# A streamed weight slice loaded in two halves: halves of its columns in place of halves of its partitions

## The chip, the cores and the metric

The kernel runs on one NeuronCore of a Trainium2 chip. The metric is device time in microseconds, the median of several executions. One more execution was taken by the hardware profiler; every duration below is from it.

## The reference: what is computed

The output is a gated mix `g * a + (1 - g) * b` of two attention layers over the same 2048 tokens of width 640, all in bfloat16; `g` is a sigmoid of `x . gate_w` for each token.

Part B (`b`) is a local attention of 32 heads of 20 columns: each token looks at itself and at seven earlier tokens, two apart.

Part A (`a`) is recurrent. The tokens are cut into 64 segments of 32. A memory of 8 rows is put in front of each segment, giving 40 rows:

```python
for s in range(n_seg):                          # 64 segments
    h = concatenate([mem, x[segment s]])        # 40 rows of 640
    q, k, v = h @ Wq, h @ Wk, h @ Wv            # 640 -> 32 heads x 192, each
    p = softmax(mask(q @ k.T * scale))
    o = (p @ v) @ Wo                            # 32 x 192 -> 640
    mem = o[:8]                                 # goes into the next segment
    outs.append(o[8:])
```

Each of Wq, Wk, Wv is 640 x 6144 and Wo is 6144 x 640, some 31 MB in all, and every segment needs all of it. The segments can't be reordered, because each one's memory comes out of the one before.

## The kernel before

The weights are cut into 80 slices of 128 partitions x 1536 columns (384 KB each). A slice of Wq, Wk or Wv is 128 rows of the contraction (`kc`, five of them) by 1536 columns (`R`, four of them: eight heads each); a row of it in memory is 3072 contiguous bytes. Wo is cut by columns into `oa` (columns 0 to 255, a slice holds six chunks of 128 rows) and `ob` (columns 256 to 639, four chunks). 67 slices stay in SBUF; they are loaded once, on SP's queue, by whole slices (`slice_tile`, L407, and `load_late`, L421). The other 13 (`stream_keys`, L374, chosen evenly over the order of use) don't fit. They are streamed again in every segment through a pool of four buffers (`wstream`, `WBUFS` = 4, tile name `wst`). Three of the streamed slices belong to Wo and are first copied to a scratch tensor `wscr` (L392), where each partition's 1536 columns lie together. Ten slices are streamed once in the prepass too.

`get_slice` (L424) hands out a slice: a resident one, one that `begin` (L439) has loaded ahead, or a new `wst` buffer with its loads. The loads of a streamed slice are two DMAs (L434 to L436). All streamed loads are issued by SP's queue, one after the other. A load's issue waits until the matmuls that read the buffer's former slice are done. Other DMAs of a segment are issued by ACT's queue in ACT's own order: `load_z` (L577, `ZQKV<-zqk_dram`, 192 KB) after the first output copy, `oz_dram` (L808), the segment's output (L833), `load_vz` (L580, `ZQKV<-zv_dram`, 96 KB) after the first transposes, `a4` (L774) and `hT` (L573).

The time is spent in part A's loop (`part_a`, L585), one pass for each segment, of which the order on PE, ACT, DVE and SP is written out by hand. On PE a pass is: `m_dense` for q and k (L588: four matmuls for each slice, one for each 32-column tile `j` of the array, 384 columns of the slice each, so that tile 0 reads columns 0 to 383, tile 3 reads 1152 to 1535); `t_qk`, transposes (L621); scores (`s_a`, `s_b`, L640 and L649); `m_v` in between; the products with v (`pv_half`, L696 and L700); then `o_group` (L726), which multiplies by Wo in 48 chunks, four at a time on the four column tiles. ACT and DVE copy PSUM to SBUF between these steps (L602, L624, L625, L709, L805, L815) and do the softmax. When two matmuls in a row use the same stationary operand, `drop_loads` (L27) removes the second weight load.

Before the loop, `part_b` computes `b` into a scratch tensor, and `prepass` computes the q, k and v parts of the 8 last rows of all segments together. After it, `part_z` (L864) computes the output rows that were held back, from slices that are still in SBUF.

Of the kernel before, what the change touches and what calls it, by code (L numbers as in the profile page):

```python
# [45 lines left out]
class _K:  # L46
# [377 lines left out]
    def get_slice(self, key):  # L424
        if key in self.res_tiles:
            return self.res_tiles[key]
        if key in self.ahead:
            return self.ahead.pop(key)
        src, split = self.slice_info(key)
        t = self.wstream.tile([128, 1536], BF, name="wst", tag="wst")  # L430
        v = t if split is None else t.rearrange("p (c f) -> p c f", c=split[0])
        if key in self.wscr:
            src = self.wscr[key].rearrange("p (c f) -> p c f", c=split[0])
        for x in range(2):  # L434
            part = slice(64 * x, 64 * x + 64)
            self.nc.sync.dma_start(v[part], src[part])  # L436
        return v

    def begin(self, *keys):  # L439
# [508 lines left out]
```

## Time and profile before

| | |
|---|---|
| runs | 2179.46, 2170.18, 2177.9 us; median 2177.9 |
| profiled execution | 2179.46 us; span from first to last instruction 2177.7 us |
| PE, matmul | 1747.3 us busy (80%) |
| DVE, ACT | 655.2 us (30%), 687.5 us (32%) |
| DMA | 434.65 MB, mean 200 GB/s; 273170 packets |
| SP's DMA queue | 183336 packets, 380.54 MB, 69.4% of 16 engines' span |
| granted TensorE clock | 0.954 |
| streamed loads | 520 of Wk, 520 of Wv, 384 of `wscr`, 260 of Wq, 192 KB each |

How to read the profile. The page lists the busy time of each engine (PE is the matmul, PEld the weight load of TensorE; POOL is GpSimd; SP issues DMAs and computes nothing) and the span in 40 equal slices, each digit a busy share in tenths. The row DMA is the mean busy share of the 16 DMA engines, GB/s is what they moved. A DMA moves its bytes as packets, one for each contiguous row here. A view by windows gives the busy time of each engine in a stretch of time (us from the start of the span), with the number of instructions in brackets, and in its last columns the granted clock, the DMA share and GB/s. A view of waits says which engine stood idle at which line until what ended: us in total, times, longest. `PE ps_d_5073 L594` is a matmul of line 594 into that PSUM tile, `SPq` the DMA queue of SP. The chain follows the work that ended last backwards, each step to what released it; a DMA in it runs from its issue to its landing.

### The profile page before, as it was taken

The numbers are of one execution on the slowest core, as the hardware profiler recorded it, in microseconds if no ns is written. First come the engines' busy times: TensorE is split into PE (matmuls) and PEld (weight loads), VectorE is DVE, ScalarE is ACT, GpSimd is POOL, SyncE is SP. The second block draws the span as 40 slices with busy tenths as digits, with TensorE's granted clock in tenths as the row PEclk, the third lists the DMA queues.
The fourth block names the chain that finished last, engine by engine and source line by source line (L and its number), as shares of the span: only waits on it lengthen the run. The fifth ranks groups of instructions, "written<-read, shape, count | busy, mean of one in ns | idle before, by whom it ended". The sixth has DMA issues, their size and how long they took to land.

```text
span 2177.7 us, 81473 instructions
## 1 busy us (share of the span) xinstructions
PE 1747.3 (80%) x42085; PEld 785.3 (36%) x30693; DVE 655.2 (30%) x1614; ACT 687.5 (32%) x1436; POOL 30.7 (1%) x62
## 2 busy tenths in 40 slices
PE   6989998777788778777877877777777787777778
PEld 3555443233333333323333333333333333333337
DVE  4555222222222232222222222222222222222221
ACT  5666221223222232222222232223223222322230
POOL 4000000000000000000000000000000000000000
PEclk9999999899998999999999999999999999999999
DMA  9111869898888899888888888889888888888891
GB/s 300 37 27 37 260 181 258 205 213 212 212 209 206 209 218 220 211 213 204 215 210 214 216 217 210 205 212 216 212 208 217 212 210 216 212 213 216 212 254 54
DMA packets 273170, 434.65 MB, mean 200 GB/s; under 512 B 101804, under 2 KB 158644, under 8 KB 272820
## 3 DMA queue, kind: packets, MB, share of 16 engines
q1 hardware_dynamic: 183336, 380.54, 69.4%
q10 hardware_dynamic: 89484, 48.90, 9.7%
q8 instruction: 286, 4.69, 1.0%
q14 instruction: 64, 0.52, 0.1%
HBM read 395.62 MB, written 34.86 MB: 198 GB/s over the span
## 4 chain that ended last, share of the span: by engine, by line
DMA 56%; PE 31%; SPq 4%; ACT 4%; issue 3%; DVE 1%; POOL 1%; ACTq 0%; DVEq 0%
DMA wst<-in_A_Wv_dram 18%; DMA ZQKV<-zqk_dram 12%; DMA wst<-in_A_Wk_dram 11%; DMA wst<-wscr 9%; PE ps_d_5073 L594 4%; SPq L436 4%; PE ps_d_5074 L732 4%; PE ps_d_5075 L732 3%; PE ps_d_5075 L594 3%; DMA ZQKV<-zv_dram 3%; PE ps_bqk L236 2%; ACT bP L259 2%; DMA wst<-in_A_Wq_dram 2%; PE ps_d_5075 L880 1%; PE ps_d_5073 L880 1%
## 5 line engine op out<-in xcount | busy, mean ns | idle before, releaser
L594 PEld LDWEIGHTS <-hT 128*32 128x32 bf16 x5632 | 163.8, 97 | 578.6 <-issue 491.2
L594 PE MATMUL ps_d_5073<-wst,hT 128*32 128x384 bf16 x1280 | 121.3, 349 | 209.0 <-DMA wst<-in_A_Wv_dram 93.2
L602 DVE CAST ZQKV<-ps_d_5075 128x768 bf16<-128x768 f32 x128 | 122.6, 958 | 291.1 <-PE ps_d_5075 L594 288.4
L732 PEld LDWEIGHTS <-ZQKV 128*32 128x32 bf16 x4608 | 138.6, 101 | 144.7 <-DMA wst<-wscr 61.0
L732 PE MATMUL ps_d_5075<-zs_4166,ZQKV 128*32 128x384 bf16 x1792 | 168.3, 357 | 0.4 <-issue 0.4
L594 PE MATMUL ps_d_5075<-wst,hT 128*32 128x384 bf16 x1024 | 91.4, 332 | 88.9 <-DMA wst<-in_A_Wv_dram 43.2
L621 PEld LDWEIGHTS <-ZQKV 128*128 128x128 bf16 x1536 | 89.0, 100 | 202.6 <-issue 156.8
L732 PE MATMUL ps_d_5074<-zs_4166,ZQKV 128*32 128x256 bf16 x2304 | 146.3, 290 | 3.8 <-issue 3.6
L625 ACT COPY ZQKV<-ps_d_5075 128x768 bf16<-128x768 bf16 x64 | 51.2, 800 | 225.1 <-PE ps_d_5075 L621 225.1
L602 DVE CAST ZQKV<-ps_d_5073 128x768 bf16<-128x768 f32 x64 | 61.3, 958 | 184.6 <-PE ps_d_5073 L594 184.6
L602 ACT CAST ZQKV<-ps_d_5074 128x768 bf16<-128x768 f32 x64 | 51.2, 799 | 205.3 <-PE ps_d_5074 L594 205.3
L732 PE MATMUL ps_d_5074<-wst,ZQKV 128*32 128x256 bf16 x768 | 78.2, 299 | 26.9 <-DMA wst<-wscr 26.0
L640 PEld LDWEIGHTS <-ZQKV 128*32 128x32 bf16 (+1 forms) x4096 | 57.6, 93 | 101.3 <-issue 65.8
L625 ACT COPY ZQKV<-ps_d_5073 128x768 bf16<-128x768 bf16 x64 | 51.2, 800 | 123.6 <-PE ps_d_5074 L669 94.5
L709 DVE CAST ZQKV<-ps_d_5073 128x192 bf16<-128x192 f32 x128 | 39.8, 353 | 162.4 <-PE ps_d_5073 L700 162.4
L709 ACT CAST ZQKV<-ps_d_5074 128x384 bf16<-128x384 f32 x64 | 30.7, 480 | 179.5 <-PE ps_d_5072 L667 85.7
L602 ACT CAST ZQKV<-ps_d_5072 128x768 bf16<-128x768 f32 x64 | 51.2, 799 | 113.3 <-PE ps_d_5072 L594 99.5
L709 DVE CAST ZQKV<-ps_d_5075 128x384 bf16<-128x384 f32 x64 | 35.7, 558 | 145.6 <-PE ps_d_5075 L700 71.1
L624 DVE COPY ZQKV<-ps_d_5074 128x768 bf16<-128x768 bf16 x64 | 35.7, 558 | 137.0 <-PE ps_d_5074 L621 137.0
L732 PE MATMUL ps_d_5075<-zv_4165,ZQKV 128*32 128x384 bf16 x1024 | 73.6, 329 | 1.6 <-issue 1.6
L696 PEld LDWEIGHTS <-ZQKV 32*128 32x128 bf16 (+1 forms) x4096 | 44.4, 101 | 79.4 <-issue 63.0
L709 ACT CAST ZQKV<-ps_d_5072 128x192 bf16<-128x192 f32 x128 | 34.7, 322 | 109.9 <-PE ps_d_5073 L700 109.9
(639 smaller groups left out, 3955.2 us busy)
## 6 DMA issues: line engine op xcount, KB each, us to landing
wst<-in_A_Wk_dram SPq DMA_DIRECT2D x520, 192.0 KB
wst<-in_A_Wv_dram SPq DMA_DIRECT2D x520, 192.0 KB
wst<-wscr SPq DMA_DIRECT2D x384, 192.0 KB
wst<-in_A_Wq_dram SPq DMA_DIRECT2D x260, 192.0 KB
zqk_dram<-zs_4166 ACTq DMA_DIRECT2D x4, 3072.0 KB
ZQKV<-zqk_dram ACTq DMA_DIRECT2D x64, 192.0 KB
zv_dram<-zv_4165 SPq DMA_DIRECT2D x32, 192.0 KB
ZQKV<-zv_dram ACTq DMA_DIRECT2D x64, 96.0 KB
```

The source lines that it names most:

```text
L236: nc.tensor.matmul(ps[:, 0:nn], lhsT=wqk[n][:, kc, 4 * g:4 * g + 4, :].rearrange("p h d -> p (h d)"), rhs=xT[:, kc, o0:o0 + nn], start=(kc ...
L259: nc.scalar.activation(Pv, ps[0:nk, :, 0:nq * nu], ACT.Exp, scale=scale_b)
L436: self.nc.sync.dma_start(v[part], src[part])
L594: mm = nc.tensor.matmul(dst[x // 2][32 * j:32 * j + 32, x % 2, 0:384], lhsT=hT[:, kc, :], rhs=sl[:, 384 * j:384 * j + 384], start=(kc == 0 ...
L602: cp(KV[:, 384 * u:384 * u + 768].rearrange("p (a f) -> p a f", a=2), ps[:, :, 0:384])
L621: nc.tensor.transpose(p[:, r, t, :], unit[2 * r + m][:, 128 * t:128 * t + 128], self.ident[:])
L625: nc.scalar.copy(KV[:, 4 * 384:6 * 384].rearrange("p (c b i) -> p c b i", b=4, i=8), blocks(pk))
L640: nc.tensor.matmul(pSs[h][32 * j:32 * j + 32, par, 40 * r:40 * r + 40], lhsT=KT[R][k0:k1, c, :], rhs=q_blocks(R)[k0:k1, :, c, :], start=(r ...
L696: nc.tensor.matmul(out[:, r, t, :], lhsT=V[2 * h + r][ks, f0:f1], rhs=E[ks, par, 40 * r:40 * r + 40], start=(r == 0 and t == 0), stop=Fals ...
L709: cp(dst, src[:, :, :, 8:40])
L732: mm = nc.tensor.matmul(b_out[part][32 * jj:32 * jj + 32, 0:n], lhsT=oTxs[2 * (R // 2) + j // 2][:, 6 * (j % 2) + 3 * (R % 2) + t, :], rhs ...
L880: nc.tensor.matmul(ps[32 * q:32 * q + 32, 0:nf], lhsT=oz[n, q][:, 24 * (R // 2) + 6 * j + 3 * (R % 2) + t, :], rhs=wo[part, c // nc_][:, c ...
```

## The change

A streamed slice is still loaded by two DMAs of 192 KB into the same buffer. Before, the first took partitions 0 to 63 with all 1536 columns and the second partitions 64 to 127. After, both take all 128 partitions: the first takes columns 0 to 767, the second columns 768 to 1535. For the slices of Wo the columns are counted in chunks (`split[0]`): three and three for `oa`, two and two for `ob`, which are 768 columns as well. A row of one DMA is 1536 bytes instead of 3072, and there are 128 of them instead of 64. A matmul contracts over all 128 partitions, so before it needed both DMAs. After, the matmuls of column tiles 0 and 1 read columns of the first DMA alone, those of tiles 2 and 3 of the second.

```diff
--- before.py
+++ after.py
@@ -432,8 +432,8 @@
         if key in self.wscr:
             src = self.wscr[key].rearrange("p (c f) -> p c f", c=split[0])
         for x in range(2):
-            part = slice(64 * x, 64 * x + 64)
-            self.nc.sync.dma_start(v[part], src[part])
+            part = slice(768 * x, 768 * x + 768) if split is None else slice(split[0] // 2 * x, split[0] // 2 * (x + 1))
+            self.nc.sync.dma_start(v[:, part], src[:, part])
         return v
 
     def begin(self, *keys):
```

## The prediction

> **What bounds the kernel now.** I read the page first: who is busy, and what the DMA engines do over the span.
>
> ```profile
> PE 1747.3 (80%) x42085; PEld 785.3 (36%) x30693; DVE 655.2 (30%) x1614; ACT 687.5 (32%) x1436; POOL 30.7 (1%) x62
> ...
> DMA  9111869898888899888888888889888888888891
> ...
> q1 hardware_dynamic: 183336, 380.54, 69.4%
> ```
>
> No engine is full, but from slice 10 to 38, the 64 segments of part A, the DMA engines are 80 to 90% busy. Next, the busy time of stretches I chose: x and B's weights (rows of 1280 B) arriving; resident slices (128 partitions, rows of 3072 B); late Wo slices (128 partitions, rows of 512 and 768 B); streamed slices; then 56 segments.
>
> ```profile
> core 0: us, PE busy (x) PEld busy (x) DVE busy (x) ACT busy (x) POOL busy (x), PEclk, DMA share, GB/s
> 5.00:10.00 5.00, 3.75 (x29) 2.74 (x30) 0.18 (x1) 2.74 (x5) 0.00 (x0) 1.00 1.00 343
> 233.00:247.00 14.00, 14.00 (x67) 6.30 (x66) 4.58 (x2) 2.11 (x2) 0.00 (x0) 1.00 1.03 396
> 360.00:370.00 10.00, 10.00 (x48) 4.51 (x46) 1.76 (x1) 2.88 (x2) 0.00 (x0) 1.00 1.00 290
> 440.00:450.00 10.00, 8.95 (x254) 3.69 (x201) 2.42 (x10) 3.31 (x10) 0.00 (x0) 0.83 1.03 235
> 500.00:2000.00 1500.00, 1174.70 (x32386) 487.79 (x22442) 421.63 (x1173) 436.18 (x1005) 0.00 (x0) 0.95 0.88 212
> ```
>
> The last two columns matter. With all 16 DMA engines full, 128-partition loads move 290 to 396 GB/s; the streamed halves, 64 partitions with the long 3072 B row, move 235 (247 in a short full stretch at 1023). The same row is 1.6 times dearer when a DMA covers half the partitions. The last row gives the segment: 1500 / 56 = 26.8 us, PE busy 1174.7 / 56 = 21.0, idle 5.8. The waits of PE in the same 56 segments say for what:
>
> ```profile
> PE ps_d_5073 L594 <- DMA wst<-in_A_Wv_dram: 86.4, 73, 4.0
> PE ps_d_5073 L594 <- DMA wst<-in_A_Wk_dram: 54.8, 55, 2.2
> PE ps_d_5073 L594 <- DMA wst<-in_A_Wq_dram: 42.4, 84, 1.7
> PE ps_d_5075 L594 <- DMA wst<-in_A_Wk_dram: 36.2, 54, 1.5
> PE ps_d_5075 L594 <- DMA wst<-in_A_Wv_dram: 27.2, 53, 1.4
> PE ps_d_5074 L732 <- DMA wst<-wscr: 23.1, 44, 1.3
> ```
>
> Together 270.1 us, 4.8 a segment: nearly all of PE's idle time is for streamed halves. The waits of SP, which issues them, over the same stretch:
>
> ```profile
> SPq L436 <- DMA ZQKV<-zv_dram: 190.9, 54, 5.4
> SPq L436 <- DMA ZQKV<-zqk_dram: 152.0, 56, 4.4
> ```
>
> A streamed half shares no data with those loads. But all DMAs of SP and ACT take turns on eight completion semaphores (283 or 284 issues on each in the trace), so an issue waits for the landing of the one eight back. 26 halves and six ACT DMAs make 32 a segment, four rounds exactly: the same half always stands behind the same load. Last, the chain, around one segment (start, us, what):
>
> ```profile
> 1014.00 5.40 DMA ZQKV<-zqk_dram
> 1019.41 3.14 DMA wst<-in_A_Wk_dram
> ...
> 1031.08 5.37 DMA wst<-in_A_Wv_dram
> 1036.49 1.47 PE ps_d_5073 L594 x13
> ```
>
> A DMA issued into a full queue takes 5.4 us; one issued when SP's wait had let the queue drain takes 3.14. That 2.3 us of standing in line recurs, and is itself made of half-rate transfers.
>
> **The change part by part.** Number, size and order of the DMAs stay (1684 of 192 KB); the shape changes.
>
> (1) Transfer. Before: 196.6 KB at 235 to 247 GB/s, 0.82 us a half. After: 128 rows of 1536 B. The trace before has no steady load of that form; 290 GB/s (rows of 512 and 768 B) bounds it below and 396 (3072 B) above, 0.68 and 0.50 us. I take 0.57, from 343 GB/s at 1280 B, the nearest row length. A segment has 26: 21.3 us become 14.8 (13.0 to 17.7). Other DMA work stays: 0.88 x 26.8 = 23.6, less 21.3, is 2.3. The DMA engines' need falls from 23.6 to 17.1 us (15.3 to 20.0), below PE's 21.0 at either end. Nothing is added to the bytes.
>
> [...]
>
> [...]
>
> (2) SP. One issue takes 465 to 588 ns at L436 (medians); 128-partition issues at L421 took 430 for plain rows and 657 for Wo in three dimensions. I take no change, 0 to +0.1 us each, at most 2.6 us a segment, hidden while SP waits 3.5 and 2.7 us a segment for the two loads above. Without that cover, the halves behind it would be late by as much; that end is inside (4).
>
> (3) Waits of PE. The first matmul of a slice waited for both halves; now column tiles 0 and 1 (in Wo: the first half of the chunks) wait for the first, 2 and 3 for the second. Behind a waiting matmul stands all of PE's queue, and behind that the evictions of ACT and DVE. The first pair can start up to one pace (0.6 us) earlier, the end still needs the second half: 0, between -0.1 and +0.05 us a slice (-1.3 to +0.65 a segment), in the same bounds. SP's reuse wait on PE splits likewise: the first half of a buffer is free two matmuls (some 0.2 us) sooner. 0.
>
> (4) The loop, by the timeline and SP's waits of one segment, from one zqk issue (1014.00) to the next (1041.61): zqk lands at +5.4 and lets a Wk half go, landed +8.55; transposes; ACT issues zv at +9.9; SP, free at +11.0, waits 3.9 and resumes at +15.0; its fourth issue is the Wv half at +17.1, landed +22.45; PE then needs 5.1 to the next zqk. With the line gone, a load takes what the drained one took: zqk 3.3 (oz goes beside it), Wk 3.1, +1.3 to zv, zv 3.3, 2.1 for SP's issues, Wv 3.1, 5.1 of PE: 21.3 instead of 27.6, 6.3 shorter. PE's own busy time in that stretch is 21.3 too. So stalls cannot all remain, and what is late next is PE itself.
>
> (5) The segment: 26.8 - 4.8 = 22.0 if all named stalls went. Two limits of almost one length take turns, and ACT's and DVE's evictions, now covered by stalls, come out in part (PE's loads already wait 38.8 us at L621 for L657, 0.7 a segment): +1.0, between 0 and 2.5 (half the stall left). The granted clock is 0.95 over the segments, 0.74 in the 5 us after the 1031-to-1036 stall, but 1.00 in the prepass where PE never rests. With fewer stalls I take half of 5% of 21.0: -0.5, between 0 and -1.0. Sum: 22.5 (21.0 to 24.5), 4.3 less, times 64: 275.
>
> (6) Start and prepass: single stalls on the stream, 7.6 us on Wv before 470 us the largest: -10 (0 to -15). Part B and the end hold no streamed slice.
>
> 2179.5 (this execution; span 2177.7) - 275 - 10 = 1894; the median of the runs is 1.6 lower: 1893. Own range: 2178 - 64 x 5.8 - 15 = 1792 to 2178 - 64 x 2.3 = 2031.
>
> **The rivals.**
> A. The stream is faster, but eight semaphores, four buffers and SP's pace stay the bound. For: SP's two waits, 6.1 us a segment; SP needs 26 x 0.57 = 14.8 more, 20.9 in all. Against: those waits are for transfers that are late through the line itself. More than half of the stall stays: 1.0 to 2.3 us gained a segment, 2114 to 2031, say 2070.
> B. The change doesn't do what it says: a row of 1536 B costs half of today's 3072 B row, as if the line were at the memory and not at the partitions. For: zqk's 1536 B rows go no faster while halves stream. Against: 396 GB/s from the same tensors, same stride. Then 0.82 us stays: 2170 to 2185.
> [...]
>
> **How the numbers follow.** Forecast 0.70, A 0.20, B 0.04, C 0.06. A measurement of this kernel tells 0.5%, 11 us. Forecast and A are faster: 0.90; B same: 0.04; C slower: 0.06. The range leaves out C and B, a tail of A above 2060 and the lowest tenth of the forecast: 1810 to 2060.
>
> **What would show it.** Packets on the first queue rise by 107776 to 291112 (rows doubled) at equal bytes. DMA share falls to some 0.76 (17.1 / 22.5) while GB/s rises to about 253 (212 x 26.8 / 22.5). The zqk and zv waits of SP fall below 2 us each; the 5.4 us pieces of the chain go to about 3.3 and PE lines rise in it; PE is busy over 90% of a segment. Wrong: a DMA share still at 0.88 (B, C), or PE still idle over 2.5 us a segment at a low share (A).

## The result, and the profile after

The changed kernel takes 1759.9 us (median of four runs, 1754.9 to 1767.1) against 2178.7 for the kernel before: a ratio of 0.8085, with a 95% interval of 0.8047 to 0.8122. The direction and the first cause of the forecast, cheaper halves, hold; the time lies 133 us under its number and 50 us under its range. The profiled execution took 1761.2 us, with a span of 1759.5.

The page of the changed kernel, the same three lines as before:

```profile
PE 1614.6 (92%) x42085; PEld 768.7 (44%) x30693; DVE 652.9 (37%) x1614; ACT 684.1 (39%) x1436; POOL 30.7 (2%) x62
...
DMA  9300185978889999889998989988989899988981
...
q1 hardware_dynamic: 291112, 380.54, 68.1%
```

The bytes are the same and the packets are 107776 more, as the doubled rows demand. The DMA engines are still 90% busy in part A, but the span has shrunk. The surprise is in the first line: PE does the same 42085 matmuls in 1614.6 us of busy time instead of 1747.3.

The window of 56 whole segments (from one zqk load to another; columns as before, the last three being granted clock, DMA share and GB/s):

```profile
core 0: us, PE busy (x) PEld busy (x) DVE busy (x) ACT busy (x) POOL busy (x), PEclk, DMA share, GB/s
459.50:1588.20 1128.70, 1051.95 (x32488) 463.05 (x22516) 420.98 (x1176) 434.65 (x1009) 0.00 (x0) 1.00 0.90 283
```

A segment is 1128.70 / 56 = 20.16 us instead of 26.8; PE is busy 18.8 of them (21.0 before) and idle 1.4 (5.8 before). So of the 6.7 us that a segment lost, 4.4 were idle time and 2.2 were busy time. 283 GB/s pass where 212 did.

The longest waits of PE in that window, and SP's longest waits, with those for the two loads that held it up before (whole span):

```profile
PE ps_d_5074 L732 <- issue: 14.9, 17, 1.6
PE ps_d_5075 L594 <- DMA wst<-in_A_Wk_dram: 7.2, 9, 1.3
PE ps_d_5073 L594 <- DMA wst<-in_A_Wk_dram: 6.5, 13, 1.2
PE ps_d_5075 L594 <- DMA wst<-in_A_Wv_dram: 6.4, 17, 1.1
...
```

```profile
SPq L436 <- DMA wst<-in_A_Wv_dram: 90.7, 108, 2.6
SPq L436 <- PE ps_d_5073 L594: 90.3, 162, 1.7
SPq L436 <- DMA wst<-in_A_Wk_dram: 83.1, 108, 3.5
...
SPq L436 <- DMA ZQKV<-zqk_dram: 7.2, 12, 1.1
...
SPq L436 <- DMA ZQKV<-zv_dram: 5.5, 7, 1.8
```

All waits of PE on `wst` in these 56 segments come to 30.7 us, 0.55 a segment, where the six rows shown before had 270. SP hardly waits for zqk and zv now. In the 56 segments it waits 240 us, 4.3 a segment, for matmuls to free a buffer; there it runs as far ahead as four buffers allow. But 168 us, 3.0 a segment, go to the landing of its own earlier halves (135 us, 2.4 a segment, from 500 to 2000 us of the kernel before): SP's and ACT's issues take turns on eight completion semaphores in this trace too, 283 or 284 on each, and an issue still waits for the DMA eight places back.

Last, the chain around one segment:

```profile
1022.56 5.83 DMA wst<-in_A_Wk_dram
1028.43 0.34 PE ps_d_5075 L594 x2
1028.82 0.43 SPq L436
1029.36 0.36 SPq L436
1029.77 4.51 DMA wst<-in_A_Wv_dram
1035.53 1.09 PE ps_d_5075 L594 x24
```

A load still takes 4.5 to 5.8 us from issue to landing. The line in front of the DMA engines didn't go away; it is only served faster. The chain of this profile can be followed back to 861 us only. In the 898 us that it covers, DMAs make some 27% of it and PE 63%; before, where it covers the whole span, they made 56% and 31%.

### The profile page after: what moved, and what is told of

Read it like the earlier page. It is cut to its first block, busy times and chain, and to the rows that moved or that the text cites. A ratio compares the mean times of both kernels' runs of the same rounds, so it can differ in the third digit from the quotient of the medians.

```text
span 1759.5 us, 80890 instructions
## 1 busy us (share of the span) xinstructions
PE 1614.6 (92%) x42085; PEld 768.7 (44%) x30693; DVE 652.9 (37%) x1614; ACT 684.1 (39%) x1436; POOL 30.7 (2%) x62
## 4 chain that ended last, share of the span: by engine, by line
PE 32%; DMA 14%; issue 2%; SPq 1%; ACT 1%; ACTq 1%; DVE 0%
PE ps_d_5073 L594 6%; DMA wst<-in_A_Wk_dram 6%; DMA wst<-in_A_Wv_dram 5%; PE ps_d_5075 L594 5%; PE ps_d_5075 L732 3%; PE ps_d_5074 L732 3%; PE ps_d_5072 L594 2%; PE ps_d_5074 L594 2%; PE ps_d_5075 L880 2%; PE ps_d_5073 L880 1%; DMA wst<-in_A_Wq_dram 1%; SPq L436 1%; DMA wst<-wscr 1%; PE ps_d_5072 L621 1%; PE ps_d_5074 L696 1%
## 5 line engine op out<-in xcount | busy, mean ns | idle before, releaser
L594 PEld LDWEIGHTS <-hT 128*32 128x32 bf16 x5632 | 160.6, 96 | 363.2 <-issue 266.3
L732 PEld LDWEIGHTS <-ZQKV 128*32 128x32 bf16 x4608 | 126.6, 96 | 109.0 <-issue 56.5
L594 PE MATMUL ps_d_5073<-wst,hT 128*32 128x384 bf16 x1280 | 128.7, 330 | 15.7 <-DMA wst<-in_A_Wk_dram 7.6
L732 PE MATMUL ps_d_5075<-zs_4166,ZQKV 128*32 128x384 bf16 x1792 | 141.4, 327 | 0.6 <-issue 0.6
L732 PE MATMUL ps_d_5074<-zs_4166,ZQKV 128*32 128x256 bf16 x2304 | 132.4, 276 | 8.8 <-issue 8.2
L602 ACT CAST ZQKV<-ps_d_5074 128x768 bf16<-128x768 f32 x64 | 51.2, 800 | 199.0 <-PE ps_d_5074 L594 179.5
L594 PE MATMUL ps_d_5075<-wst,hT 128*32 128x384 bf16 x1024 | 101.9, 328 | 25.2 <-DMA wst<-in_A_Wv_dram 17.4
L625 ACT COPY ZQKV<-ps_d_5075 128x768 bf16<-128x768 bf16 x64 | 51.2, 800 | 119.0 <-PE ps_d_5075 L621 119.0
L625 ACT COPY ZQKV<-ps_d_5073 128x768 bf16<-128x768 bf16 x64 | 51.2, 800 | 95.4 <-PE ps_d_5074 L669 45.9
L640 PEld LDWEIGHTS <-ZQKV 128*32 128x32 bf16 (+1 forms) x4096 | 53.6, 92 | 64.4 <-issue 34.8
L602 ACT CAST ZQKV<-ps_d_5072 128x768 bf16<-128x768 f32 x64 | 51.2, 800 | 70.0 <-DMA wst<-in_A_Wv_dram 38.7
L732 PE MATMUL ps_d_5075<-zv_4165,ZQKV 128*32 128x384 bf16 x1024 | 71.4, 326 | 2.1 <-issue 2.0
L709 ACT CAST ZQKV<-ps_d_5074 128x384 bf16<-128x384 f32 x64 | 30.7, 480 | 92.3 <-PE ps_d_5072 L667 77.9
L259 ACT ACTIVATE bP<-ps_bS 128x968 bf16<-128x968 f32 (+1 forms) x80 | 64.8, 856 | 3.9 <-PE ps_bS L254 3.8
```

Of the source, the lines that this page charges most:

```text
L259: nc.scalar.activation(Pv, ps[0:nk, :, 0:nq * nu], ACT.Exp, scale=scale_b)
L594: mm = nc.tensor.matmul(dst[x // 2][32 * j:32 * j + 32, x % 2, 0:384], lhsT=hT[:, kc, :], rhs=sl[:, 384 * j:384 * j + 384], start=(kc == 0 ...
L602: cp(KV[:, 384 * u:384 * u + 768].rearrange("p (a f) -> p a f", a=2), ps[:, :, 0:384])
L625: nc.scalar.copy(KV[:, 4 * 384:6 * 384].rearrange("p (c b i) -> p c b i", b=4, i=8), blocks(pk))
L640: nc.tensor.matmul(pSs[h][32 * j:32 * j + 32, par, 40 * r:40 * r + 40], lhsT=KT[R][k0:k1, c, :], rhs=q_blocks(R)[k0:k1, :, c, :], start=(r ...
L709: cp(dst, src[:, :, :, 8:40])
```

## The experiments

Theory P: what pays is that each DMA covers all 128 partitions. Rival W: what pays is the other half of the edit, that column tiles 0 and 1 can start before the slice is complete. Theory S, formed after the result, is on the surprise: stalls lengthen PE's busy time too.

**The early start taken away (second_first).** The changed kernel, with the half that the first matmul needs issued last:

```diff
-        for x in range(2):
+        for x in (1, 0):
```

> The changed kernel with the two column halves issued in the other order: columns 768 to 1535 first, columns 0 to 767 second. The first matmul of a slice (column tile 0) now waits for the half that is issued last, so nothing of a slice can start before all of it has landed; the transfers stay the same. Theory P (it is the 128-partition shape of each DMA that pays): 1760 to 1775 us, PE's waits on wst up by less than 20 us in all. Rival W (it is the early start of column tiles 0 and 1 that pays): 0.5 to 0.8 us come back for each slice that PE waits for, 13 a segment at most, so 1850 us or more.

1758.4 us (1752.1 to 1759.9); on its own chip a ratio of 0.8116 (0.8095 to 0.8137) to the kernel before, where the changed kernel has 0.8085 (0.8047 to 0.8122). PE's waits on `wst` rise from 30.7 to 43.1 us in 56 segments, and nothing comes of it in the time. Rival W falls: the halves' separate waits are worth nothing here that can be measured.

**One DMA for a slice (whole_slice, and again beside the changed kernel).**

```diff
-        for x in range(2):
-            part = slice(768 * x, 768 * x + 768) if split is None else slice(split[0] // 2 * x, split[0] // 2 * (x + 1))
-            self.nc.sync.dma_start(v[:, part], src[:, part])
+        self.nc.sync.dma_start(v[:], src)
```

> The changed kernel with one DMA for a streamed slice: 128 partitions, all 1536 columns, rows of 3072 B, 384 KB. It has the row length of the kernel before, the partition span of the changed kernel and no early start. Theory P: rows of 3072 B as cheap as the resident ones (396 GB/s), SP issues 13 instead of 26 a segment, 1745 to 1790 us. Rival W: PE waits for whole slices as in the kernel before, 1850 us or more. Rival C (short rows): if 1536 B rows cost extra, this is clearly faster than the changed kernel, under 1740 us.

> The changed kernel unaltered, on the same chip as the next two, so that their difference is read directly: 1750 to 1770 us.

> One DMA of 384 KB for a streamed slice again, beside the changed kernel on one chip. If the 2% of the first comparison is real: 1715 to 1735 us, 25 to 45 us under the changed kernel.

1724.1 us in the first comparison. That is under the 1745 to 1790 us expected, and in the range put down for dear short rows (under 1740). On one chip: the changed kernel 1753.9 us, ratio to the kernel before 0.8035 (0.8008 to 0.8062); whole slices 1723.3 us, ratio 0.7888 (0.7862 to 0.7913). The gain of some 2% is real, and this version beats both kernels. No half at all is needed, which speaks against W a second time. The window of 56 segments of the version with whole slices:

```profile
457.00:1557.00 1100.00, 1031.85 (x32488) 453.24 (x22512) 421.32 (x1176) 434.33 (x1009) 0.00 (x0) 1.00 0.89 290
```

19.64 us a segment; the DMA engines need 0.89 x 19.64 = 17.5 us, against 0.90 x 20.16 = 18.1 with halves. Rows of 3072 B are thus a little cheaper than twice as many of 1536 B, though with (17.5 - 2.2) / 13 = 1.18 us a slice (334 GB/s; the 2.2 us of other DMA work are from the kernel without a stream below) not as cheap as the 396 expected. SP also issues half as often and waits 1.4 us a segment for its own loads to land instead of 3.0, and PE's waits on `wst` fall to 6.6 us. Which of these makes the 2% wasn't separated.

**Rows halved once more (rows_768).**

```diff
+        if split is None:
+            v4, s4 = (a.rearrange("p (j f) -> p j f", f=384) for a in (v, src))
+        else:
+            v4, s4 = v, src
         for x in range(2):
-            part = slice(768 * x, 768 * x + 768) if split is None else slice(split[0] // 2 * x, split[0] // 2 * (x + 1))
-            self.nc.sync.dma_start(v[:, part], src[:, part])
+            self.nc.sync.dma_start(v4[:, x::2, :], s4[:, x::2, :])
```

> The changed kernel with halves made of every other 384 columns (column tiles 0 and 2, then 1 and 3; in Wo every other chunk): still two DMAs of 192 KB over 128 partitions, but rows of 768 B (512 B in slices of the first 256 columns of Wo), twice as many. Theory P: a row's price follows its bytes (768 B rows took half of 1536 B rows in the first traces), the DMA need rises by 5 to 20% from the 290 GB/s that such rows made before, 1770 to 1850 us. Rival C: each row costs a fixed amount and this doubles it again; DMA share at 1.0 and over 1900 us.

1812.4 us (1805.4 to 1817.9), ratio 0.8361 (0.8330 to 0.8392). The packets of SP's queue rise to 539432, the DMA need to 19.3 us a segment (0.92 of 20.94). Short rows cost, but only 6% more need for twice the rows: a row's price is nearly its bytes. A half takes (19.3 - 2.2) / 26 = 0.66 us here, still under the 0.82 us of the kernel before.

**The disputed price alone (late_low_first, late_mid_first).** 25 resident slices that are loaded before the prepass, each in halves of 64 partitions. In dispute is why streamed halves move 235 GB/s where whole resident slices move 396: by P1 it is which partitions one DMA touches, P2 and P3 are the rivals below. The two kernels differ in which partitions go first (the diff is the first one's; the other has `[[(32, 96)], [(0, 32), (96, 128)]]`):

```diff
+        todo = []
...
-            self.nc.sync.dma_start(v, src)
             self.res_tiles[k] = v
+            todo.append((v, src))
+        for group in [[(0, 64)], [(64, 128)]] if part == 0 else [[(0, 128)]]:
+            for v, src in todo:
+                for a, b in group:
+                    self.nc.sync.dma_start(v[a:b], src[a:b])
```

> The changed kernel with the 25 slices of the first late load (before the prepass) each loaded in two DMAs of 64 partitions: all low halves (partitions 0 to 63) first, then all high halves. No PE work waits for them in between, so the DMA rate at full share is read directly between 230 and 275 us. [...] Rival P2 (the streamed halves were slow because low and high halves alternate, or because of the PE's reads): 380 GB/s or more.

> As the former, but the first DMA of each slice takes partitions 32 to 95, and the rest (0 to 31 and 96 to 127) follow in a second pass. The first pass has the same DMAs as to size (192 KB), row count (64) and row length (3072 B); only the partitions differ. [...] Rival P3 (64 rows in one DMA are too few for 16 engines, four each): 230 to 250 GB/s in the first pass too.

The whole kernels take 1774.1 and 1780.9 us (one execution each). Windows of the first pass, partitions 0 to 63 first:

```profile
core 0: us, PE busy (x) PEld busy (x) DVE busy (x) ACT busy (x) POOL busy (x), PEclk, DMA share, GB/s
235.00:240.00 5.00, 4.95 (x24) 2.29 (x24) 0.66 (x1) 1.86 (x1) 0.00 (x0) 1.00 1.06 205
240.00:245.00 5.00, 5.00 (x25) 2.28 (x24) 2.29 (x1) 0.00 (x0) 0.00 (x0) 1.00 1.05 202
245.00:250.00 5.00, 4.95 (x24) 2.25 (x23) 0.00 (x0) 1.86 (x1) 0.00 (x0) 1.00 1.05 207
```

and partitions 32 to 95 first:

```profile
230.00:235.00 5.00, 5.00 (x25) 2.29 (x24) 0.61 (x1) 1.83 (x1) 0.00 (x0) 1.00 0.93 298
235.00:240.00 5.00, 4.95 (x24) 2.26 (x24) 1.68 (x1) 1.44 (x1) 0.00 (x0) 1.00 0.87 294
240.00:245.00 5.00, 5.00 (x25) 2.25 (x23) 2.13 (x1) 0.42 (x1) 0.00 (x0) 1.00 0.82 262
```

The same 192 KB, the same 64 rows of 3072 B: 204 GB/s with the engines full, against up to 298 with the engines not even full. The first is under the 235 of the streamed halves, the second under the 396 of whole slices. In the second, SP issued one such DMA only every 0.64 us, which is 307 GB/s at most; the price itself is in the packet records of the trace. A 3072 B packet takes 251 ns (median; mean 249) for partitions 0 to 63 and 121 ns (mean 146) for 32 to 95. In the changed kernel, which loads these slices whole, it is 121 ns (mean 126). With a mean of 146 ns, 16 engines move 337 GB/s at most, so the issue alone didn't keep the second kernel from 396. The means of 249, 146 and 126 ns leave most of the price to which partitions a DMA touches, and little to its size or the number of its rows: P2 and P3 fall. Low halves alone are even dearer than low and high in turn (200 ns in the loop of the kernel before).

The second passes add little. The high halves, 64 to 127, moved 200 to 213 GB/s with the engines full, as dear as the low ones. The pieces 0 to 31 and 96 to 127 moved 207 to 213 GB/s at a DMA share of 0.70 to 0.74: SP issued one of these 96 KB DMAs every 0.465 us, which is 211 GB/s, so they don't tell the price with the engines full.

What makes 0 to 63 and 64 to 127 dear and 32 to 95 not is not shown by these runs.

**PE's busy time without stalls (no_stream, before_six).** In both, streamed slices are replaced by resident ones of the same matrix after the first segment: all 13 in the changed kernel, seven of 13 in the kernel before (there the diff's last condition is `i % 2 == 0`).

```diff
+        if key in self.alias:
+            return self.res_tiles[self.alias[key]]
...
+            gone = [k for i, k in enumerate(k for k in self.slice_keys() if k in self.stream_keys) if True]
+            self.alias = {k: next(r for r in self.res_tiles if r[0] == k[0] and r not in self.late[LATE[2]:])
+                          for k in gone if k not in self.ahead}
...
```

> The changed kernel with nothing streamed in the loop: after the first segment the 13 streamed slices are replaced by resident slices of the same matrix, so the loads are left out and the products use other weights. It shows the loop without the stream. If TensorE's busy time were fixed work, as the prediction took it (21.0 us a segment less 0.5), the segment could not be under some 21 us and the whole not under 1800. Theory S (stalls themselves lengthen TensorE's busy time, by the halved clock and by matmul pipelines that drain and fill): busy time is 18.3 to 18.8 us a segment, the segment 19.0 to 19.8, the whole 1690 to 1740 us.

> The kernel before (halves of 64 partitions) with only six of the 13 streamed slices streamed after the first segment; the other seven are replaced by resident slices of the same matrix, so their loads are left out and the products use other weights. The dear shape stays, the need falls: 12 x 0.82 + 2.3 = 12.1 us of DMA a segment. Theory S with P: the stalls go, and TensorE's busy time falls from 21.0 to 18.3 to 18.9 us a segment although no column half is used; 1690 to 1770 us. Rival W: PE still waits for whole slices, six a segment, at 0.5 us or more, and busy time stays near 20: over 1830 us.

1615.9 us (1615.3 to 1618.2) and 1647.9 (1643.4 to 1650.0). Both are under what was expected. The windows of 56 segments, without the stream and with six slices in halves of 64 partitions:

```profile
446.00:1460.90 1014.90, 1006.17 (x32488) 440.49 (x22516) 420.45 (x1176) 433.30 (x1008) 0.00 (x0) 1.00 0.12 32
```

```profile
456.70:1479.80 1023.10, 1010.52 (x32488) 444.92 (x22512) 420.54 (x1176) 434.82 (x1009) 0.00 (x0) 1.00 0.61 161
```

The loop without a stream takes 18.12 us a segment with PE busy 17.97: that is the work. With six slices in the dear shape, busy time is 18.05 and the segment 18.27, though a matmul there still needs both halves of its slice. So the 21.0 us of the kernel before hold 3 us that are no work, and they leave when the stalls leave, in the dear shape too. The DMA traffic doesn't order the busy times: 18.43 us with whole slices at 290 GB/s, 19.28 with rows of 768 B at 272, 21.0 in the kernel before at 212.

**What a stall costs (one_stall, short_stall).** In the changed kernel, the last output copy of a segment is repeated, which holds PE up at L745 (nine times in one kernel, three times in the other):

```diff
-                nc.scalar.copy(whi[:, 256:640], b_out["ob"][:, 0:384])
+                for _ in range(9):
+                    nc.scalar.copy(whi[:, 256:640], b_out["ob"][:, 0:384])
```

> The changed kernel with the last output copy of a segment on ScalarE (479 ns) made nine times instead of once, which holds TensorE up at one place in each segment by some 3.2 to 3.8 us; DMAs as they were. Theory S: TensorE's clock is halved after such a stall and its busy time rises from 18.8 to 19.3 to 20.1 us a segment, so the segment grows by more than the stall itself or by as much with stalls elsewhere swallowed; granted clock under 0.97; 1960 to 2060 us. Rival (busy time is fixed work): 18.8 us a segment, granted clock unchanged at 0.99, 1965 to 2000 us.

> The changed kernel with the last output copy of a segment made three times instead of nine, a stall of TensorE of some 0.6 to 1.0 us in each segment. Theory S: too short to halve the clock, granted clock 0.98 or more, busy time 18.6 to 19.1 us a segment, 1800 to 1830 us. Rival: any stall halves the clock; granted clock 0.95 or less, and over 1850 us.

2052.8 us and 1778.4 us (one execution each). PE's wait at that place (whole span) and the window of 56 segments, nine copies:

```profile
PE ps_d L745 <- ACT ZQKV L816: 245.8, 63, 5.2
```

```profile
475.20:1857.00 1381.80, 1132.28 (x32488) 456.32 (x22514) 422.52 (x1176) 650.04 (x1457) 0.00 (x0) 0.91 0.74 231
```

and three copies:

```profile
463.10:1605.30 1142.20, 1045.24 (x32488) 451.31 (x22513) 420.79 (x1176) 487.05 (x1121) 0.00 (x0) 1.00 0.89 279
```

One stall of 245.8 / 63 = 3.9 us drops the clock from 1.00 to 0.91 and raises busy time from 18.8 to 20.2 us; the segment grows by 4.5 us, to 24.67, though waits elsewhere shrink. A stall of 0.9 us (51.2 us in 57 waits) leaves the clock at 1.00 and adds only 0.24 us to the segment (0.34 against the changed kernel on the same chip), less than was expected; the busy time doesn't rise (18.7). Theory S holds for the clock. The kernel before had no stall over 4.0 us, but strings of them. Two stretches of it:

```profile
1030.19:1036.49 6.30, 3.28 (x135) 1.77 (x115) 2.68 (x9) 1.55 (x6) 0.00 (x0) 0.94 0.92 235
1036.49:1041.61 5.12, 5.12 (x144) 2.56 (x115) 0.95 (x5) 1.49 (x5) 0.00 (x0) 0.74 0.91 222
```

In the first PE was busy 3.28 of 6.30 us and no single wait was over 1.4 us; in the next 5 us the clock was 0.74. It is no exception: the 36 records of half clock in 56 segments of that kernel last 3.41 or 6.83 us each, and ahead of every one PE had been busy for 24 to 59% of the last 3.4 us, with no idle gap over 2.7 us.

The clock records of the kernel before and of the changed one show only 1.0 and 0.5. The half clock doesn't need one long stall: the kernel before ran at 0.74 after a string of waits of at most 1.4 us each. What decides between the two clocks is not shown.

**A resident slice in place of a buffer (whole_s12).** Whole slices, one streamed slice fewer, one buffer fewer, and fewer loads ahead in the prepass:

```diff
-N_STREAM = 13
+N_STREAM = 12
-WBUFS = 4
+WBUFS = 3
...
-        for k in keys:
+        for k in keys[:max(0, WBUFS - len(self.ahead))]:
...
-                    self.begin(*streamed("v", 2), *streamed("v", 3))
+                    pass
...
-                    self.begin(*streamed("k", 0, 1)[0:2])
+                    pass
...
-                        self.begin(*streamed("k", 0, 1)[2:3], *streamed("k", 2, 3))
+                        pass
```

> One DMA for a streamed slice, and the fourth buffer of the stream holds one more resident slice instead: 12 slices streamed, three buffers; of what the prepass loaded ahead only its first group is still loaded ahead. The DMA need falls by a thirteenth (17.4 to some 16.2 us a segment). Theory N (the need, close to the segment's length, sets the rest of the stalls): 1690 to 1725 us. Rival L (latency: a load takes some 4 us and three buffers are too few to cover it): 1750 us or more, with a lower DMA share and more waits of PE on wst.

1828.3 us (1820.2 to 1842.0), slower than with 13 slices and four buffers. PE's longest waits in 56 segments:

```profile
PE ps_d L592 <- DMA wst<-in_A_Wk_dram: 38.5, 57, 2.4
PE ps_d L592 <- DMA wst<-in_A_Wv_dram: 25.1, 50, 1.5
PE ps_d L730 <- DMA wst<-wscr: 13.0, 15, 1.8
```

80.8 us of waits on `wst` in place of 6.6, at a lower DMA share (0.84): rival L. The DMA need is 0.84 x 20.59 = 17.3 us, not the 16.2 expected. A segment is 20.59 us against 19.64, some 56 us over 62 passes; another 42 us are lost before them (the loop's first zqk load is issued at 459.1 us instead of 417.3), where the loads ahead are missing. In this arrangement, in which the choice of streamed slices shifts too, the fourth buffer is worth more than one more resident slice.

## Why the prediction was right and wrong

**The bound, part (1): right.** The half's price falls from 0.82 us to (18.1 - 2.2) / 26 = 0.61 us, where 2.2 us is the other DMA work as the kernel without a stream shows it. 0.57 was taken from the 1280 B row, between bounds of 0.50 and 0.68. That the partitions are the cause is shown by the two late-load kernels. Shorter rows cost a little: the need is 18.1 us with rows of 1536 B against 17.5 with 3072 B.

**SP, part (2): wrong sign, small.** An issue was taken as unchanged or dearer; the medians are 366 to 426 ns instead of 466 to 588.

**The waits, part (3): right.** Taken as nothing; swapping the halves changes nothing.

**The loop, part (4): right in what it shortens, wrong in how.** SP's waits for zqk and zv fall from 6.1 to 0.2 us a segment. But loads were to land in 3.1 to 3.3 us with the line gone. They take 4.5 to 5.8 in the chain: SP, free of those waits and quicker to issue, fills the line again. That costs PE little, 0.55 us a segment of waits on `wst`, because SP mostly runs ahead of need.

**The segment, part (5): this is the step that failed.** It gave 22.5 us: 20.5 of PE's busy time and 2.0 of idle time. Measured: 18.8 and 1.4. The term for returning stalls (+1.0) was too large by 0.6. The term for busy time was -0.5, bounded by -1.0, and measured -2.2. It counted the clock alone, as half of 5% of 21.0, and had no term for the busy time that a stall costs at full clock; the rest of the 21.0 us was kept as work, where the loop without a stream needs 17.97.

The records of the trace tell roughly how the 2.2 us divide. In the kernel before, 2.57 us of PE's busy time a segment lay in records of half clock, after the change 0.08. If a matmul takes twice as long there, 1.28 us of a segment were lost before and 0.04 after: some 1.2 us are the clock's, over twice the term. The rest, some 1.0 us, is busy time at full clock. Matmuls overlap: a record of L594 lasts 322 ns or more, but in the loop without a stream 32488 matmuls make 1006.17 us of PE's busy time, some 31 ns each, 0.12 us for four. The first four after an idle gap of over 0.15 us add 0.34 us in the kernel before and 0.36 after. With 7.5 such gaps at full clock in a segment before and 2.1 after, that is 1.6 us too much against 0.5. Both shares are estimates, and the ends of matmuls are modelled in the profile.

The gaps are not the whole account. In the kernels above whose clock was 0.998 or more, busy time rises with the number of gaps, but not strictly: 17.97 us at 0.3 gaps a segment (no stream), 18.05 at 0.5 (six slices), 18.43 at 1.9 (whole slices), 18.54 at 2.3 (halves swapped), 18.66 at 2.4 (three copies), 18.78 at 2.1 (the changed kernel), 19.28 at 3.3 (rows of 768 B). Three buffers, at a clock of 0.996, have 18.67 at 3.1. What else sets it stays open.

**Start and end, part (6).** Outside the 62 passes between the loop's first and last zqk load, 5 us were gained; the forecast had some 19 there with the first and last pass. The 62 passes gave 413 us instead of 267, and that is the miss.

**The rivals.** A (latency, buffers and SP's pace stay the bound) was given 0.20 and didn't come; its ingredients are real, as the run with three buffers and SP's 3.0 us a segment of waits for its own halves show. B and C (C: the kernel slower) are excluded by the late loads and by the rows of 768 B: a streamed half over 128 partitions took 0.66 us even with rows of 768 B, against 0.82 in the kernel before. What would show it: packets right, DMA share wrong (0.90 instead of 0.76), because the need was 18.1 us and not 17.1 and the segment it is divided by 20.2 and not 22.5; 283 GB/s instead of 253; the waits for zqk and zv under 2 us and PE's share over 90% right.

**What stays over.** The loop without a stream is 18.12 us, so the changed kernel still pays 2.0 us a segment for it and whole slices pay 1.5.

## What to carry to other kernels

Cut a load along its columns, or not at all, before cutting it along partitions: two DMAs of 64 partitions each, 0 to 63 and 64 to 127, moved 235 GB/s here where the same bytes over 128 partitions took 0.61 us a half, some 320 GB/s. When a change removes stalls of TensorE, don't keep its busy time as a floor: part of it is the stalls' own doing (here 3 of 21.0 us a segment, by estimate some 1.2 us of them half clock, and 0.22 us more for the first four matmuls after each gap), and a run with the awaited loads left out gives the real floor for the price of one kernel. A freed queue fills again (in the chain a load takes 4.5 to 5.8 us from issue to landing after the change, 5.4 before); what a faster transfer buys is seen in who waits, not in the time from issue to landing.

## What the runs showed of the hardware that was not expected

SP's issue depends on the DMA's shape: 466 to 588 ns (medians) for 64 partitions, 366 to 426 ns for 128 partitions with half the columns, 326 to 332 ns for whole slices. 64 partitions in the middle (32 to 95) were issued only every 0.64 us, but their packets took 121 ns where those of partitions 0 to 63 took 251 (medians).

A 3.9 us stall of TensorE once in a segment of some 20 us cost 4.5 us, and one of 0.9 us 0.2 to 0.4. Half clock needs no long stall: in the kernel before it came after 3.4 us in which PE was busy for 24 to 59%, with no gap over 2.7 us.
